# Batch 1 of a fused attention and MLP kernel: segment layout with VectorE turns and GpSimd sums, in place of TensorE transposes

## Chip, cores, metric

One Trainium2 chip, one core. The metric is device time in microseconds of one execution, the median of several runs. Every kernel was timed in rounds against the kernel before on the same chip. "Faster" or "slower" needs 2%.

## The reference

```python
# q, k, v: (8, 8, 576, 64) f32: batch, heads, tokens, head width
q_lm = q.reshape(B, H, 32, 18, D).mean(axis=3)        # 32 landmarks, each the mean of a segment of 18 tokens
k_lm = k.reshape(B, H, 32, 18, D).mean(axis=3)
A, Bm, C = sm(q, k_lm), sm(q_lm, k_lm), sm(q_lm, k)   # sm: softmax of the scaled product
Z = Bm.T / (norm1(Bm) * norminf(Bm))
for _ in range(6):
    Z = 2 * Z - Z @ Bm @ Z                            # pseudo-inverse of Bm, step by step
x = heads_side_by_side(A @ Z @ C @ v)                 # (8, 576, 512)
xn = (x - mean(x)) / sqrt(var(x) + 1e-6) * g_ln
out = x + relu(xn @ w_ch1) @ w_ch2                    # 512 -> 2048 -> 512
```

The eight batches are independent up to `x`. The MLP runs over blocks of 128 tokens, four blocks to a group, and a block can start when its tokens are out of the attention. TensorE therefore always has two streams: attention of a coming batch, and the MLP of batches already done, which the code puts between attention steps with `fill(n)`.

## The kernel before: the parts that matter here

There are two ways to make the attention's operands. Batches 0 and 1 are loaded in a layout that TensorE transposes (`pst`, nine in 0.67 us at 28.07 us), and TensorE sums the landmarks too (`pss`). Batches 2 to 7 are loaded in the segment layout, where a partition holds one head's one segment. VectorE turns such a tile (`STREAM_TRANSPOSE` of 128x576, 0.76 us each in the trace). The k landmarks are summed on VectorE (`add_up`) and the q landmarks on GpSimd, called POOL here (in batches 5 to 7 the k landmarks too).

```python
def load_seg(src, b, u, queue, turned=False):          # segment layout
    t = stage.tile([P, SEG, D], FP32, name="stg", tag="stg")
    rows = src[b, 4 * u:4 * u + 4].rearrange("h (l j) d -> (h l) j d", j=SEG)
    for o, i_ in ((0, 64), (64, 0)) if turned else ((0, 0),):
        n = 64 if turned else P                        # turned: two DMAs of 64 partitions
        keep(queue.dma_start(out=t[ds(o, n), :, :], in_=rows[ds(i_, n), :, :]))
    return t

class Coming:                                          # a set of coming batches, segment layout
    def load(self, i, queue=nc.sync):
        ...
        self.stg[i] = load_seg(..., turned=(nm == "v" and u % 2 == 1))   # v of odd units is turned
    def cast(self, i):
        ...
        pool.tensor_copy(out=t[:], in_=stg[:])         # f32 -> f16
        if nm == "q" or self.k_by_pool:                # landmark sum: five adds on POOL
            for o, x, y in (...):
                pool.tensor_tensor(out=o, in0=x, in1=y, op=ALU.add)

def attention(bs):                                     # batches 0 and 1
    ...
    for j in range(NJ):
        TR(pst[:, j, :], n16[:, j, :, :], ident16[:])  # nine transposes to a tile ...
    dve.tensor_copy(out=t[:], in_=pst[:])              # ... and a copy (VectorE or ScalarE)
    sums()                                             # nine matmuls for the landmarks: pss
    yield

def attention2(bs, c):                                 # batches 2 to 7
    psb = p1([P, W, LM], "psb")                        # first scores: lmq and lmk must be there
    ...

# order of the program
for i in range(HID // W1N):
    load_w1(i)
load_v(1)
...
scale_w1(0, (1, 2, 3)); ...; scale_w1(1); scale_w1(2)  # W1 times g, mostly on POOL
run(a0); fill(4); run(a1); fill(4); ...                # a0, a1: attention of batches 0 and 1, step by step
cast_v(1)
fetch_w2()                                             # 16 loads, 16 casts on POOL
run(a1); fill(16); settle()
sets = [Coming((2,)), Coming((3, 4)), Coming((5, 6), True), Coming((7,), True)]
for i, _ in enumerate(a1):
    fill(5 if i < 9 else 7)
    ...
```

The output stores go through the same SP queue as the loads. The kernel does not hold them to program order (no `keep` around them): the compiler places them.

The softmax here doesn't subtract the row's maximum and nothing guards it: scores larger than these inputs give would overflow.

Of the kernel before, what the change touches and what calls it, by code (L numbers as in the profile page):

```python
# [16 lines left out]
P = 128  # L17
# [3 lines left out]
def kernel(  # L21
# [35 lines left out]
    nat = ctx.enter_context(tc.tile_pool(name="nat", bufs=8))  # L57

# [28 lines left out]
    raw = {0: {}, 1: {}}  # L87

    def load_qk(b):
        for u in range(U):  # L90
            raw[b]["q", u] = load(q, b, u, nc.sync)
            raw[b]["k", u] = load(k, b, u, nc.sync)

    def load_v(b):
        for u in range(U):
            raw[b]["v", u] = load(v, b, u, nc.sync)
# [12 lines left out]
    def cast_qk(b, u, nm, engine):  # L109
        t = nat.tile([P, NJ, 2, D], FP16, name="nat", tag="nat")  # L110
        engine.tensor_copy(out=t[:].rearrange("p j r d -> p r j d"), in_=raw[b][nm, u][:])
        nat_tiles[b, nm, u] = t

    def cast_v(b):
        natv_of[b] = natv = natv_buf[b % NV]
        for u in range(U):
            pool.tensor_copy(out=natv[:, 2 * u:2 * u + 2, :, 0:D], in_=raw[b]["v", u][:])
# [6 lines left out]
    keep(nc.sync.dma_start(out=g_sb[:], in_=moe_g_ln.rearrange("(c p) -> p c", p=P)))  # L124
# [5 lines left out]
    make_identity(nc, ident16)  # L130

# [51 lines left out]
    cast_v(0)  # L183
    bones = const.tile([P, 4, 32], FP16, name="bones")
    for u in range(U):
        for nm in ("q", "k"):
            cast_qk(0, u, nm, dve)
        if u == 0:

            dve.tensor_copy(out=bones[:], in_=mask4[:, :, None].broadcast_to([P, 4, 32]))  # L190
            for i, t in enumerate(zcbd_buf):
                dve.tensor_copy(out=t[:, :, D], in_=(mask4t if i in (3, 5) else mask4)[:])


    load_qk(1)
    for u in range(U):
        for nm in ("q", "k"):
            cast_qk(1, u, nm, pool)

# [3 lines left out]
    xpool = ctx.enter_context(tc.tile_pool(name="xpool", bufs=16))  # L203
# [14 lines left out]
    def scale_w1(i, by=(0, 1, 2, 3)):  # L218
        for c in by:
            o, i_ = w1_16[:, c, ts(i, W1N)], w1_stg[i, c // 2][:, ts(c % 2, W1N)]  # L220
            if c == 0:
                dve.tensor_scalar(out=o, in0=i_, scalar1=g_sb[:, c:c + 1],
                                  scalar2=None, op0=ALU.mult)
            else:
                pool.tensor_scalar(out=o, in0=i_, scalar1=g_sb[:, c:c + 1],
                                   scalar2=0.0, op0=ALU.mult, op1=ALU.add)
# [10 lines left out]
    for i in range(HID // W1N):  # L237
        load_w1(i)
    load_v(1)


# [242 lines left out]
    class Coming:  # L484
        def __init__(self, bs, k_by_pool=False):
            self.bs, self.k_by_pool = bs, k_by_pool
            self.units = [(b, u) for b in bs for u in range(U)]
            pairs = [(w, w + 1) for w in range(0, len(self.units), 2)]
            self.parts = [(nm, w) for pair in pairs for nm in ("k", "q") for w in pair]
            self.parts += [("v", w) for w in range(len(self.units))]  # L490
            self.jobs = []
            for i, (nm, w) in enumerate(self.parts):
                if nm != "v":
                    self.jobs.append((self.turn, i))
                if nm == "k" and not k_by_pool:
                    self.jobs.append((self.add_up, i))
            self.done, self.turned, self.lms = 0, set(), []
            self.stg, self.n16, self.sums, self.xT, self.lm = {}, {}, {}, {}, {}
# [22 lines left out]
        def cast(self, i):  # L521
# [7 lines left out]
            if nm == "v":  # L529
                natv_of[b] = natv_buf[b % NV][:].rearrange("p a j e -> p (a j) e")  # L530
                assert b - NV in v_used
                pool.tensor_copy(out=natv_of[b][:, ds(SEG * u, SEG), 0:D], in_=stg[:])
                return
# [3 lines left out]
            if nm == "q" or self.k_by_pool:  # L537
                s = asum.tile([P, NJ, D], FP32, name="asum", tag="asum")
                s16 = asm.tile([P, D], FP16, name="s16", tag="s16", bufs=8)
                self.sums[i] = s16  # L540
                for o, x, y in ((s[:], t[:, 0:9, :], t[:, 9:18, :]),
                                (s[:, 0:4, :], s[:, 0:4, :], s[:, 4:8, :]),
                                (s[:, 0:2, :], s[:, 0:2, :], s[:, 2:4, :]),
                                (s[:, 0, :], s[:, 0, :], s[:, 8, :]),
                                (s16[:], s[:, 0, :], s[:, 1, :])):
                    with nc.allow_low_precision("sums are rounded once, to fp16"):
                        pool.tensor_tensor(out=o, in0=x, in1=y, op=ALU.add)
# [264 lines left out]
    def store(j, ot, cols=ds(0, DM), queues=(nc.sync, nc.sync)):  # L812
        for i in range(2):
            b, c = divmod(2 * j + i, NJ)
            half = ot[ds(64 * i, 64), cols]
            if b < 2:
# [126 lines left out]
    a0, a1 = attention((0,)), attention((1,))  # L943

    def run(*who):
        for a in who:
            next(a)

    warm(50, 128)
    for _ in range(4):  # L950
        run(a0)
        warm(3, 256)
    run(a0)
    warm(1, 512)
    run(a0)
    warm(1, 512)
    run(a0)
    warm(2, 512)
    for it in range(6):
        run(a0)  # L960
        warm(1, 512)
        if it == 5:
            scale_w1(0, (0,))
    run(a0)
    warm(2, 512)
    run(a0, a0)
    warm(3, 512)
    run(a1)
    warm(1, 512)
    scale_w1(0, (1, 2, 3))  # L970
    fill(1)
    warm(2, 512)
    fill(1)
    warm(2, 512)
    scale_w1(1)
    scale_w1(2)
    run(a0)
    fill(4)
    run(a1)
    fill(4)  # L980
    run(a0)
    fill(2)
    run(a1)
    fill(4)
    for _ in a0:
        pass
    fill(2)
    run(a1)
    fill(4)
    run(a1)  # L990
    fill(4)
    cast_v(1)
    fetch_w2()
    run(a1)
    fill(16)
    settle()


    sets = [Coming((2,)), Coming((3, 4)), Coming((5, 6), True), Coming((7,), True)]
# [11 lines left out]
    def next_cast():  # L1011
        if to_cast:
            c, i = to_cast[0]
            nm, w = c.parts[i]
            if nm != "v" or c.units[w][0] - NV in v_used:
                to_cast.pop(0)
                if cast_before:
                    next_load()
                cast_before.append(i)
                c.cast(i)  # L1020

    for _ in range(6):
        next_load()
    for i, _ in enumerate(a1):
        fill(5 if i < 9 else 7)
        settle()
        next_cast()
        if 5 <= i < 11:
            sets[0].next_job()
    for _ in range(2):  # L1030
        sets[0].next_job()


    counts = [[8, 13, 9] + 6 * [7] + [5] + 3 * [6] + 2 * [9],
              [10, 10, 9, 9, 9, 9] + [9, 9, 8, 8, 8, 8] + [8] + [8, 8, 6, 5] + 6 * [9],
              [12, 12, 15, 15, 15, 13] + 6 * [11] + [10] + 10 * [8],
              [14, 21, 21] + 6 * [10] + [10] + 5 * [9]]
    for c, after, count in zip(sets, sets[1:] + [None], counts):
        for step, _ in enumerate(attention2(c.bs, c)):
            fill(count[step])  # L1040
            settle()
            if late and step >= 3:
# [4 lines left out]
            if after and step >= (5 if after.k_by_pool else 1):  # L1047
# [37 lines left out]
```

## Time and profile before

| | kernel before |
|---|---|
| time, median of 4 runs beside the changed kernel | 330.38 us (329.90 to 331.06) |
| span of the profiled run | 328.4 us |
| TensorE busy | 314.6 us (96%) |
| TensorE idle between 20 and 60 us | 4.26 us |
| mean granted clock | 1.00 |
| batch 1's first scores (`psb`) on TensorE | 37.16 us |
| batch 2's first scores | 63.30 us |
| POOL's first batch-2 cast, its 16th q or k cast | 47.74, 80.70 us |
| wait of TensorE for `xnT` near 142 us | 1.04 us |

Idle time is the stretch less the busy time. These are the engine busy times of the kernel before by longer stretches; the columns are the ones that the prediction explains, TensorE first.

```profile
20.00:60.00 40.00, 35.74 (x448) 24.32 (x448) 32.17 (x72) 20.42 (x39) 35.82 (x58) 1.00 1.05 361
60.00:100.00 40.00, 39.05 (x512) 18.93 (x510) 33.08 (x76) 30.58 (x73) 37.94 (x46) 1.00 0.84 255
100.00:140.00 40.00, 39.09 (x557) 19.38 (x555) 29.93 (x61) 19.14 (x42) 37.32 (x51) 1.00 0.67 185
140.00:170.00 30.00, 28.96 (x515) 13.91 (x513) 12.16 (x29) 14.04 (x30) 22.10 (x33) 1.00 0.55 118
```

TensorE is idle for 4.26, 0.95, 0.91 and 1.04 us in them.

### The profile page before, as it was taken

What the parts mean: (1) busy time and instruction counts of PE and PEld (TensorE: products, weight loads), DVE (VectorE), ACT (ScalarE), POOL (GpSimd) and SP (SyncE); (2) the same over time, 40 slices, a digit from 0 to 9 for tenths busy, and PEclk for the clock granted to TensorE, in tenths of its full rate; (3) what the DMA queues carried; (4) which work ended last, traced back from release to release, by engine and by line L of the source; (5) the groups of instructions that cost most, each with busy time, mean ns of one, the idle gap of its engine ahead of it and who ended that gap; (6) DMA issues with size and microseconds to landing.
All of it is one profiled execution on the core that took longest, in us unless ns stands there. A gap on an engine that the chain in (4) does not pass through costs nothing.

```text
span 328.4 us, 8241 instructions
## 1 busy us (share of the span) xinstructions
PE 314.6 (96%) x3408; PEld 163.0 (50%) x3408; DVE 176.7 (54%) x396; ACT 150.9 (46%) x304; POOL 154.6 (47%) x240
## 2 busy tenths in 40 slices
PE   8879899999999999989999999999999999999995
PEld 8537764454445544434545445454444444444443
DVE  2658869879966588864228568822557120010012
ACT  2426762739961561867304664364046107305600
POOL 3489889999999999989900025200014000000000
PEclk9999999999999999999999999999999999999999
DMA  7999999998598683698022203230242125032023
GB/s 276 350 361 360 383 401 291 317 359 250 212 209 226 186 225 109 163 278 128 4 66 59 43 16 80 66 66 2 64 103 27 32 64 98 0 72 60 0 49 79
DMA packets 36917, 50.34 MB, mean 153 GB/s; under 512 B 18320, under 2 KB 22672, under 8 KB 36880
## 3 DMA queue, kind: packets, MB, share of 16 engines
q1 hardware_dynamic: 36720, 49.69, 53.1%
q8 instruction: 26, 0.43, 0.6%
q10 hardware_dynamic: 160, 0.13, 0.2%
q14 instruction: 11, 0.09, 0.1%
HBM read 36.70 MB, written 9.44 MB: 141 GB/s over the span
## 4 chain that ended last, share of the span: by engine, by line
PE 58%; POOL 17%; DVE 6%; DMA 4%; issue 3%; ACT 2%; SPq 0%; POOLq 0%
PE psh L73 27%; PE pso L73 25%; POOL asum L67 9%; POOL nat L67 4%; POOL natv L67 2%; DMA out_dram<-ot 2%; POOL xn L67 2%; PE psy L73 1%; ACT xn L67 1%; DMA stg<-in_v_dram 1%; PE pscv L73 1%; DVE xT L67 1%; DVE ebd L67 1%; POOL s L67 1%; DMA xnT<-xn 1%
## 5 line engine op out<-in xcount | busy, mean ns | idle before, releaser
L73 PE MATMUL psh<-xnT,w 128*128 128x512 f16 (+1 forms) x640 | 134.2, 358 | 1.0 <-DMA xnT<-xn 1.0
L73 PE MATMUL pso<-w,hT 128*128 128x512 f16 (+1 forms) x592 | 133.0, 374 | 0.0
L67 ACT ACTIVATE hT<-psh 128x512 f16<-128x512 f32 x144 | 84.7, 597 | 94.8 <-PE psh L73 94.6
L73 PEld LDWEIGHTS <-w 128*128 128x128 f16 x640 | 59.4, 98 | 56.0 <-issue 3.0
L73 PEld LDWEIGHTS <-hT 128*128 128x128 f16 x592 | 56.0, 98 | 57.8 <-issue 0.9
L67 DVE SCALAR_TENSOR_TENSOR ot<-pso,rstd,xblk 128x512 f32<-128x512 f32 (+1 forms) x37 | 27.1, 732 | 79.0 <-PE pso L73 78.9
L67 POOL CAST nat<-stg 128x1152 f16<-128x1152 f32 x28 | 32.9, 1185 | 3.8 <-DMA stg<-in_k_dram 1.2
L67 POOL TENSOR_TENSOR asum<-asum 128x256 f32<-128x256 f32 (+2 forms) x54 | 28.3, 523 | 4.2
L67 DVE TENSOR_TENSOR xblk<-psy,rcpd 128x512 f32<-128x512 f32 (+1 forms) x40 | 27.6, 691 | 1.7
L67 POOL TENSOR_TENSOR asum<-nat 128x576 f32<-128x576 f16 x18 | 24.9, 1381 | 1.5
L67 DVE SCALAR_TENSOR_TENSOR st<-st,psn 128x192 f16<-128x192 f16 (+3 forms) x36 | 14.2, 395 | 19.1 <-PE psn L73 19.1
L67 POOL TENSOR_SCALAR xn<-xblk,mvg 128x512 f16<-128x512 f32 x14 | 9.6, 695 | 30.3 <-ACT junk L67 30.3
L67 POOL CAST natv<-stg 128x1152 f16<-128x1152 f32 x16 | 18.1, 1150 | 9.6 <-DMA stg<-in_v_dram 9.6
L67 POOL TENSOR_SCALAR negm<-mvg 128x1 f32<-128x1 f32 x14 | 2.7, 191 | 41.7 <-DVE mvg L67 40.2
L67 DVE TENSOR_TENSOR ebd<-st,mask 128x256 f16<-128x256 f16 (+1 forms) x30 | 21.4, 715 | 1.0
L67 DVE STREAM_TRANSPOSE xT<-nat 128x576 uint32<-128x576 uint32 x24 | 18.2, 760 | 0.8 <-POOL nat L67 0.8
L73 PE MATMUL psy<-zcbd,ea 128*128 128x260 f16 (+1 forms) x80 | 15.9, 276 | 1.3 <-DVE zcbd L67 1.1
L67 ACT ACTIVATE ea<-psea 128x576 f16<-128x576 f32 x12 | 7.2, 648 | 17.8 <-PE psea L73 17.8
L73 PE MATMUL idle<-zeros 128*128 128x128 f16 (+2 forms) x82 | 14.0, 325 | 1.1 <-DVE eps_ln L167 1.1
L73 PEld LDWEIGHTS <-ea 128*128 128x128 f16 (+1 forms) x80 | 7.3, 100 | 11.9 <-issue 4.2
L67 DVE RECIPROCAL rcpd<-psy 128x8 f32<-128x8 f32 (+1 forms) x40 | 7.8, 195 | 9.9 <-PE psy L73 9.6
L67 ACT ACTIVATE junk<-xblk 128x512 f16<-128x512 f32 x14 | 8.8, 625 | 9.3 <-DVE xblk L67 9.1
(109 smaller groups left out, 265.5 us busy)
## 6 DMA issues: line engine op xcount, KB each, us to landing
stg<-in_q_dram SPq DMA_DIRECT2D x16, 576.0 KB, 6.2
stg<-in_k_dram SPq DMA_DIRECT2D x16, 576.0 KB, 6.0
out_dram<-ot SPq DMA_DIRECT2D x70, 128.0 KB, 2.4
stg<-in_v_dram SPq DMA_DIRECT2D x10, 576.0 KB, 8.2
w1stg<-in_moe_w_ch_dram SPq DMA_DIRECT2D x16, 256.0 KB, 6.0
w2stg<-in_moe_w_ch_dram SPq DMA_DIRECT2D x16, 256.0 KB, 5.4
stg<-in_v_dram SPq DMA_DIRECT2D x12, 288.0 KB, 5.7
xnT<-xn SPq DMA_TRANSPOSE x28, 3.2
```

The lines of the kernel that those rows point to most:

```text
L67: return lambda *args, **kw: keep(getattr(self.engine, op)(*args, **kw))
L73: keep(nc.tensor.matmul(o, l, r, start=start, stop=stop, tile_position=(rb, cb), skip_group_check=(skip or cb != 0)))
```

## The change

The intent: TensorE is the full engine, so take batch 1's 72 transposes and landmark matmuls off it and give the work to VectorE (turns) and POOL (sums), as in the later batches. The start is tidied too: the g vector is loaded by rows and transposed on TensorE, half of a v cast goes from POOL to ScalarE (ACT), and so do 14 W1 scalings, six from POOL and all eight of VectorE. Not shown below are new fill counts of the later sets. The core of the diff, cuts marked:

```diff
-    keep(nc.sync.dma_start(out=g_sb[:], in_=moe_g_ln.rearrange("(c p) -> p c", p=P)))
+    g_rows = xpool.tile([P, DM], FP32, name="g_rows", tag="xblk")[0:KCH, 0:P]
+    keep(nc.sync.dma_start(out=g_rows, in_=moe_g_ln.rearrange("(c p) -> c p", p=P)))
...
-            if c == 0:
-                dve.tensor_scalar(out=o, in0=i_, scalar1=g_sb[:, c:c + 1], ...)
+            if c == 0 or c == 1 and i != 1 and i != 2:
+                act(o, i_, AF.Copy, scale=g_sb[:, c:c + 1])
...
-    a0, a1 = attention((0,)), attention((1,))
+    a0 = attention((0,))
+    sets = [Coming((1,), ""), Coming((2,), "q", 6), Coming((3, 4)), Coming((5, 6), "qk", 5),
+            Coming((7,), "qk", 5)]
...
+    fill(4); s1.next_job(); fill(8); s1.next_job()      # turns on VectorE
+    for _ in a0: pass
+    fill(4); s1.next_job(); s1.next_job(); fill(2)
+    for i, (nm, w) in enumerate(s1.parts):
+        if nm == "q":
+            s1.sum_by_pool(i)                           # two landmark sums, after the W1 scalings
+            ...
+    for _ in range(2):                                  # v casts of batch 1
+        c, i = to_cast.pop(0)
+        c.cast(i)
+    fill(4)
...
     fetch_w2()
     for _ in range(6):
         next_load()
-    counts = [[8, 13, 9] + 6 * [7] + [5] + 3 * [6] + 2 * [9],
+    counts = [[12, 8, 10] + 6 * [5] + [5] + 5 * [7],
+              [8, 13, 9] + 6 * [7] + [5] + 3 * [6] + 2 * [9],
```

(The added lines of the order of the program are put together here. In `counts`, each number is how many MLP matmul groups follow an attention step.)

## The prediction

> **What bounds the kernel now.** I read the page's busy shares first, then the engine busy times by stretch of 10 us, then the order of time on TensorE and on GpSimd, then the chain that ended last and the packed DMA records.
>
> ```profile
> PE 314.6 (96%) x3408; PEld 163.0 (50%) x3408; DVE 176.7 (54%) x396; ACT 150.9 (46%) x304; POOL 154.6 (47%) x240
> ...
> 20.00:30.00 10.00, 8.08 (x88) 5.45 (x88) 8.16 (x19) 3.44 (x7) 9.42 (x19) 1.00 1.10 349
> 30.00:40.00 10.00, 8.58 (x138) 7.24 (x137) 8.01 (x21) 7.88 (x15) 9.05 (x15) 1.00 1.05 383
> ...
> 130.00:140.00 10.00, 10.00 (x54) 5.11 (x53) 8.43 (x20) 7.34 (x21) 9.69 (x14) 1.00 0.65 171
> ```
>
> The columns of the stretches are PE, weight load, DVE, ACT, POOL, clock, DMA share, GB/s. TensorE is busy 96% of the span, so the end is set by its work plus its few idle spots. But POOL's 47% is an average of two halves: it is full (9.0 to 9.7 of 10) from 20 to 140 us and nearly idle afterwards. The DMA share is about 1 up to 50 us. There are therefore three limits early on, and only TensorE late.
>
> ```profile
> 24.45 0.42 PE L73 MATMUL pss<-pm,nat 128*128 128x64 f16 x9
> ...
> 28.07 0.67 PE L77 MATMUL pst<-ident,nat 128*128 128x128 f16 x9
> 28.57 0.43 PE L73 MATMUL pss<-pm,nat 128*128 128x64 f16 x9
> 28.84 1.04 PE L73 MATMUL psh<-xnT,w 128*128 128x256 f16 x8
> ...
> 37.16 0.22 PE L73 MATMUL psb<-klm,qbd 64*32 64x32 f16 x8 [0.84 <-DVE qbd L67]
> ```
>
> Batch 1's transposes (pst) and landmark sums (pss) stand here between MLP matmuls (psh); nine of each take 0.77 us from start to next start (28.07 to 28.84). The batch's first scores (psb) begin at 37.16 us, after 44 of the 128 narrow psh matmuls of the first block group.
>
> ```profile
> 21.50 11.91 POOL L67 TENSOR_SCALAR w<-w1stg,g_sb 128x256 f16<-128x256 f32 x24
> 33.78 1.15 POOL L67 CAST natv<-stg 128x1152 f16<-128x1152 f32 x1 [0.38 <-DMA stg<-in_v_dram]
> 35.28 1.15 POOL L67 CAST natv<-stg 128x1152 f16<-128x1152 f32 x1 [0.35 <-DMA stg<-in_v_dram]
> 36.37 10.53 POOL L67 CAST w<-w2stg 128x512 f16<-128x512 f32 x16
> 47.74 1.15 POOL L67 CAST nat<-stg 128x1152 f16<-128x1152 f32 x1 [0.84 <-PE psn L73]
> 51.83 1.32 POOL L67 TENSOR_TENSOR asum<-nat 128x576 f32<-128x576 f16 x1
> 53.23 1.66 POOL L67 TENSOR_TENSOR asum<-asum 128x256 f32<-128x256 f32 x3
> 54.96 0.32 POOL L67 TENSOR_TENSOR s<-asum 128x64 f16<-128x64 f32 x1
> ...
> 139.19 2.84 DMA xnT<-xn
> 142.17 1.02 PE psh L73 x4
> ```
>
> POOL's order in time shows the program order that the change cuts into: W1 scaling, v casts, W2 casts, batch 2. One landmark sum is the five adds from 51.83 to 55.28, about 3.5 us with gaps. The last two lines are from the chain: until 139 us the chain runs through POOL, and TensorE waits 1.04 us for its product at 142.17. POOL is a second bound with no slack.
>
> [...] the old g load left 512 packets of 4 bytes, took 9.7 us to land, and the DMA rate fell from about 405 GB/s to 66 GB/s for a microsecond near 13 us in the packet records. [...] here 72 transposes need eight copies (three on DVE at 746 ns, five on ACT at 1111 ns). [...] No pair of equal adds is in this trace; its 128x576 add took 1381 ns.
>
> **The change part by part.**
>
> 1. TensorE, batch 1. Removed after 27.2 us: three pst/pss groups (0.77, 0.76, about 0.9 with the copy wait left out), psb and psc 0.84 (37.16 to 38.00), psse and pscv 1.00 (41.59 to 42.59), psn, psa and pszc about 1.6: 5.9 us. Added, read from batch 2, which has this form already: psb and psec 1.13 (its 0.38 us of waiting left out), psse 0.13, pscv 1.19 and 0.75 less tails = 1.8, psea 0.64, six psn and pszc about 0.7: 4.4 us. Net -1.5 us on the full engine. The first transpose group lay among filler matmuls and counts nothing.
>
> 2. The start. In DVE's order, zcbd of batch 0 stands behind a W1 scaling that waited 0.93 us for W1 data at 21.10. The scaling goes to ACT, and half of batch 0's last v cast too (it held pscv 0.51 us at 14.59). I take -1.2 us for the first MLP matmul (27.2 to about 26.0). The g load's hole is worth about 1.2 us of DMA time to everything behind it: the last W1 piece lands at about 31.1 instead of 32.3.
>
> 3. POOL. Two landmark sums are added, 2 x 3.5 = +7.0 us. Six scalings go to ACT, 6 x 0.50 = -3.0; half of a v cast, -0.6. Casts of batch 1 stay. Net about +3.5 us on an engine with no slack.
>
> 4. Where the added sums lie. In program order they come behind the last W1 scaling. That needs the last W1 piece, so the three scalings saved don't bring it forward by more than the DMA does: 31.1 + 2 x 0.5 = 32.1. Sums end at 32.1 + 7.0 = 39.1; the small DVE turns bring psb of batch 1 to about 39.6, where it was 37.16. By then 40 psh matmuls stand before it in TensorE's order instead of 44. TensorE is idle for much of the time before: from 26.0 to 39.6 it has only 40 x 0.109 + 1.6 for psxt and psy = 6.0 us of useful work, and the long wait for q sums is not filled. ACT, which gets 14 scalings (about 0.40 us, estimated from 0.26 us for 128 and 0.65 us for 576 columns), four centerings at most and the ReLUs, runs to about 35 us and isn't the last.
>
> 5. Balance for TensorE at the end of batch 1: psb later by 39.6 - 37.2 = +2.4; four narrow matmuls fewer done, +0.4; work from psb on 4.4 against 3.4 (0.84 + 1.0 + 1.6), +1.0: about +3.8 us behind.
>
> 6. POOL behind that: v casts end at 41.4, W2 casts at 41.4 + 10.5 = 51.9 against 46.9; the waits of 0.84 and two of 0.28 us that it had before batch 2's casts go away, so the lag is about 4 us. It has little to give back until 140 us, so the xnT at 142.17 is late by much the same 4 us. The two lags are not added: TensorE is late by 3.8 when it comes to wait for it.
>
> After 142 us both versions have the same MLP work (13.81 us per 64 matmuls) and the same attention. The sum is 330.5 + 4 = 334.5 us.
>
> **The rivals.**
>
> A: TensorE's saving comes through. If the q sums are early enough, or the retuned fill counts cover them, what remains is -1.5 (work) - 1.2 (start) - about 1 (the old stalls of 0.58 and 0.84 at 33.9 and 37.16 go away): 326.5 to 327 us. For it speaks the 96% of TensorE, and that the fill counts were clearly set by hand: twelve steps of MLP are put behind psb, which one would rather put ahead of it had it been seen waiting. Against it speaks POOL's order of time.
>
> B: POOL becomes the bound up to 140 us, twice: at psb of batch 1 and at the xnT near 142 us. That is the sum above, 334.5 us. [...]
>
> C: the POOL lag is absorbed. POOL's casts also wait for buffers that DVE frees at TensorE's pace; then only the first lag counts, less slack, and the start pays for some of it: about 331.5 us.
>
> D: ACT becomes the bound in 22 to 40 us by its scalings and ReLUs. It had 7.88 of 10 busy in 30 to 40 already. It would hold psh by 1 to 2 us, but psb waits longer for POOL, so it adds nothing to B.
>
> **Range and chances.** My working says B; the hand-set counts speak for A or C, and my error on the POOL end time is some 2 us. Weighing B at 50%, C at 30%, A at 20% gives 334.5 x 0.5 + 331.5 x 0.3 + 326.8 x 0.2 = 332.1, so 332 us, range 326 to 337. Faster than 323.9 us would need more than A gives: 6%. Slower than 337.1 needs B with slow adds: 10%. Within 2%: 84%.
>
> **What would show it right or wrong.** Right: in TensorE's order of time psb of batch 1 starts near 39.6 us after a wait of 3 us or more for a landmark turn or s16; POOL's ten adds end near 39 us; W2 casts end near 52 us; a wait on xnT of more than 1 us near 145 us; first MLP matmul near 26 us; no 4-byte hole in the DMA. Wrong: psb starts before 37.5 us, or the waits at xnT vanish although POOL's W2 casts end 4 us later (then C), or TensorE's waits before 65 us sum to less than before (then A).

(Statements on the hardware that no trace or run of this case shows are cut out, here and in the expectations of e0 and e10. No term of the sum is among them: it came to 330.5 + 4 = 334.5 us. What is gone with them is a case of rival B, 336 to 338 us, for adds on POOL that are slower than the shortest of 1.27 us; the 10% for "B with slow adds" rests on it (1381 ns in the prediction is the mean of POOL's 18 adds of 128x576). The reason given for slow adds was not shown, and in the changed kernel's first profile batch 1's two 128x576 adds took 1.27 us each (34.03 and 37.51 us).)

## The result

The changed kernel took **339.47 us** (337.41 to 342.04, 4 runs) beside 330.38 us of the kernel before. The ratio is 1.028, 95% interval 1.0225 to 1.0336: slower. The prediction said 332.0 with a range up to 337.

The profiled run of the changed kernel is its slowest, 342.04 us; the repeat e0_after gives a profile of an ordinary one, and I name it where they differ. First the page of the changed kernel: busy line, and of the 40 slices (8.5 us each) TensorE and its clock.

```profile
PE 316.3 (93%) x3424; PEld 162.1 (48%) x3424; DVE 178.9 (53%) x396; ACT 155.0 (46%) x318; POOL 156.1 (46%) x245
...
PE   8876299899999998969999999999999999999995
...
PEclk9999679999999999998999999999999999999999
```

TensorE's busy time did not fall, it rose by 1.7 us, and slice 5 (34 to 42.5 us) is nearly empty. The clock row has a 6 and a 7 right there. The stretches of the changed kernel, short ones first:

```profile
30.00:40.00 10.00, 2.75 (x32) 2.16 (x31) 5.16 (x9) 6.23 (x15) 7.25 (x12) 0.84 1.04 276
40.00:50.00 10.00, 8.80 (x161) 6.26 (x161) 5.98 (x18) 4.36 (x10) 9.84 (x18) 0.65 0.64 214
```

```profile
20.00:60.00 40.00, 28.38 (x423) 19.75 (x416) 25.30 (x56) 21.84 (x47) 31.80 (x52) 0.87 0.96 301
60.00:100.00 40.00, 38.37 (x425) 18.68 (x423) 35.46 (x75) 25.73 (x59) 34.27 (x45) 1.00 0.83 238
100.00:140.00 40.00, 38.76 (x638) 18.42 (x637) 29.48 (x60) 18.48 (x38) 37.16 (x49) 1.00 0.82 207
140.00:170.00 30.00, 26.74 (x261) 12.49 (x259) 16.25 (x39) 20.30 (x49) 27.91 (x42) 0.94 0.75 163
```

Idle is now 11.62, 1.63, 1.24 and 3.26 us: 7.4 us more before 60 us, 2.2 us more around the `xnT` product, 1.0 us between. With the 1.7 us of extra busy time (mostly matmuls at a lower clock) that makes 12.3 us, close to the 11.9 us by which the span grew (340.3 against 328.4); outside these stretches it idles a little less. Between 30 and 40 us TensorE was busy 8.58 us before, 2.75 us now. Of these 5.8 us, 2.2 are the transposes and sums that left. The larger part, 4.1 us, is MLP matmuls (`psh`: 5.98 us before, 1.91 now): they were ready, but in program order they now stand behind the scores that TensorE waits for. So the work that left had filled waits, and nothing was put in its place.

TensorE's order of time in the changed kernel (start, length, what; in brackets the idle time before it and who ended it):

```profile
37.73 0.24 PE L74 MATMUL psb<-lmk,lmq 32*32 32x32 f16 x8 [3.54 <-DVE lmq L68]
41.20 0.22 PE L74 MATMUL psb<-lmk,lmq 32*32 32x32 f16 x4 [3.23 <-DVE lmq L68]
...
41.27 1.13 PE L74 MATMUL psec<-xT,lmq 32*32 32x512 f16 x28
42.34 5.10 PE L74 MATMUL psh<-xnT,w 128*128 128x256 f16 x24
...
152.51 3.21 PE L74 MATMUL psh<-xnT,w 128*128 128x512 f16 x8 [3.26 <-DMA xnT<-xn]
```

The narrow `psh` that follow batch 1's first scores in the kernel before:

```profile
38.00 3.67 PE L73 MATMUL psh<-xnT,w 128*128 128x256 f16 x32
```

Two waits of over 3 us stand before batch 1's scores. After them everything on TensorE is slow: 28 `psec` take 1.13 us, and 24 narrow `psh` take 5.10 us, that is 213 ns each, where the kernel before took 3.67 us for 32, 115 ns each. The same happens at 152.51 us. This is the step that I had not thought of at all. In the trace the granted clock falls to 0.50 at both places: from 36.9 to 47.1 us, that is 2.7 us into the wait of 3.54 us (0.65 on average between 40 and 50 us), and from 152.9 to 156.3 us, 0.4 us after the end of the wait for `xnT` of 3.26 us. In the run e1 below it is down from 32.4 to 35.8 us. How long a wait brings it down is not one number here. Over all profiled runs, 14 waits at the `xnT` product lasted 2.69 to 3.26 us; after 12 the clock fell, after two (2.92 us in e16, 2.94 in e9) it did not, and after none of those up to 1.83 us. Early in e1 it fell with no wait above 2.06 us: TensorE was busy 0.93 of the 3.5 us from 29.0 to 32.5 us, and the clock was 0.50 after that. In e17 it was busy the same 0.93 us, with the same wait of 2.06 us, and the clock stayed at 1.00. What decides between the two, no run shows.

POOL's order of time in the changed kernel:

```profile
33.13 0.93 POOL L68 TENSOR_SCALAR w<-w1stg,g_sb 128x256 f16<-128x256 f32 x2 [1.91 <-DMA w1stg<-in_moe_w_ch_dram]
34.03 1.27 POOL L68 TENSOR_TENSOR asum<-nat 128x576 f32<-128x576 f16 x1
...
40.58 0.32 POOL L68 TENSOR_TENSOR s<-asum 128x64 f16<-128x64 f32 x1
40.85 2.23 POOL L68 CAST natv<-stg 128x1152 f16<-128x1152 f32 x2
43.02 9.17 POOL L68 CAST w<-w2stg 128x512 f16<-128x512 f32 x16
52.61 1.15 POOL L68 CAST nat<-stg 128x1152 f16<-128x1152 f32 x1 [0.42 <-DMA stg<-in_k_dram]
...
85.57 1.15 POOL L68 CAST nat<-stg 128x1152 f16<-128x1152 f32 x1 [3.52 <-DMA stg<-in_q_dram]
```

The last W1 piece reached POOL at 33.13 us after a wait of 1.91 us; I had put its landing at 31.1. Part of the reason may be seen in the packet records. v of batch 1 now comes in the segment layout, and its odd unit is "turned": two DMAs of 64 partitions. While they are in flight the 4608-byte packets of v take 364 to 465 ns (medians by microsecond, 31 to 34 us) in place of 182, the 2048-byte packets of the W2 load 155 to 158 ns (32 to 34 us) in place of 87, and the rate falls to 173 to 197 GB/s between 31 and 34 us from about 390. The kernel before shows the same drop (229 to 246 GB/s between 52 and 57 us, 406 at 50 us), when batch 2's turned v comes in. It was there to be seen. But it does not explain the 2 us: the ordinary run e0 has the same slow stretch (143 to 195 GB/s; 279 on average from 30 to 40 us, in the first profile 276, in the kernel before 383), and there the last W1 scaling begins at 31.74 us. The rest belongs to this slow run alone, and its cause is open.

The lag of POOL against the kernel before is 4.9 us at batch 2's first cast (52.61 against 47.74) and 9.6 us at its 16th q or k cast (90.28 against 80.70). It grows on the way (in e0 less, from 4.9 to 7.0 us). One place stands out, the wait of 3.52 us for a load at 85.57 (in e0 1.11 us). The SP queue's order of time in the changed kernel, then in the kernel before:

```profile
67.80 7.37 SPq L813 DMA_DIRECT2D out_dram<-ot  x6
75.27 1.30 SPq L106 DMA_DIRECT2D stg<-in_k_dram  x1
```

```profile
63.54 1.25 SPq L817 DMA_DIRECT2D out_dram<-ot  x2
64.89 0.53 SPq L105 DMA_DIRECT2D stg<-in_q_dram  x1
```

Six output stores, each waiting for its MLP result, now stand in the queue ahead of loads that POOL needs. So there are four suspects: the waits and the clock, the split v load, POOL's added sums, and the stores ahead of the loads. What each is worth can't be read from one trace, since POOL and TensorE wait for each other.

### The profile page after: what moved, and what is told of

Its sections match the earlier page's. It is cut to its first block, busy times and chain, and to the rows that moved or that the text cites. A ratio compares the mean times of both kernels' runs of the same rounds, so it can differ in the third digit from the quotient of the medians.

```text
span 340.3 us, 8292 instructions
## 1 busy us (share of the span) xinstructions
PE 316.3 (93%) x3424; PEld 162.1 (48%) x3424; DVE 178.9 (53%) x396; ACT 155.0 (46%) x318; POOL 156.1 (46%) x245
## 4 chain that ended last, share of the span: by engine, by line
PE 58%; POOL 20%; DMA 13%; DVE 4%; issue 2%; SPq 1%; POOLq 0%; DVEq 0%
PE psh L74 28%; PE pso L74 25%; POOL asum L68 11%; DMA stg<-in_v_dram 6%; POOL nat L68 5%; DMA w1stg<-in_moe_w_ch_dram 4%; POOL natv L68 2%; POOL xn L68 2%; PE pscv L74 2%; PE psy L74 1%; DMA stg<-in_q_dram 1%; POOL s L68 1%; DMA xnT<-xn 1%; DVE ebd L68 1%; DMA w2stg<-in_moe_w_ch_dram 1%
## 5 line engine op out<-in xcount | busy, mean ns | idle before, releaser
L74 PE MATMUL psh<-xnT,w 128*128 128x512 f16 (+1 forms) x640 | 136.6, 366 | 3.8 <-DMA xnT<-xn 3.3
L74 PEld LDWEIGHTS <-w 128*128 128x128 f16 x640 | 61.3, 100 | 60.3 <-DMA xnT<-xn 3.6
L68 POOL TENSOR_TENSOR asum<-asum 128x256 f32<-128x256 f32 (+2 forms) x60 | 31.6, 527 | 4.7
L68 POOL TENSOR_TENSOR asum<-nat 128x576 f32<-128x576 f16 x20 | 26.9, 1346 | 1.5
L68 POOL TENSOR_SCALAR xn<-xblk,mvg 128x512 f16<-128x512 f32 x14 | 9.7, 693 | 32.5 <-ACT junk L68 32.5
L68 POOL CAST natv<-stg 128x1152 f16<-128x1152 f32 (+1 forms) x16 | 17.7, 1118 | 11.1 <-DMA stg<-in_v_dram 8.8
L68 DVE STREAM_TRANSPOSE xT<-nat 128x576 uint32<-128x576 uint32 x28 | 21.2, 761 | 0.2 <-POOL nat L68 0.2
L68 ACT ACTIVATE ea<-psea 128x576 f16<-128x576 f32 x14 | 8.3, 648 | 21.0 <-PE psea L74 21.0
L74 PEld LDWEIGHTS <-ea 128*128 128x128 f16 (+1 forms) x80 | 7.5, 101 | 11.5 <-issue 3.8
```

Source lines behind the costliest of these rows:

```text
L68: return lambda *args, **kw: keep(getattr(self.engine, op)(*args, **kw))
L74: keep(nc.tensor.matmul(o, l, r, start=start, stop=stop, tile_position=(rb, cb), skip_group_check=(skip or cb != 0)))
```

## The experiments

All have 3 rounds (e12 5), on three chips, each beside the kernel before on the same one, and it took 330.2 to 330.5 us. "Net lateness" below is the start of batch 2's first scores less 63.30 us (kernel before), less 1.73 us for the eight more `pso` matmuls (0.216 us each) that the changed kernel's fill counts put ahead of that point: work done early is not time lost.

### e0_after: the changed kernel again

No edit.

> The changed kernel again, as the yardstick for the runs of this call. Both theories: 337 to 342 us, 1.02 to 1.035 of before. If its runs again spread over 4 us or more while before spreads over 1 us, the spread belongs to the kernel, which the clock theory explains [...] and the theory of late sums alone does not.

339.21 us (337.62 to 340.83), 1.027 (1.0231 to 1.0308). Its profile has the two waits at `psb` at 1.96 and 3.08 us, net lateness 6.3 us, and the `xnT` wait again 3.26 us with slow `psh` after it. In the slowest run, profiled first, the net lateness was 8.9 us. The runs spread over 3.2 us and those of the kernel before over 0.7, a little under the 4 us that I had set as the sign of the clock theory (that the waits lower the clock, and so cost twice). TensorE, then POOL's last W1 scaling, in e0:

```profile
36.53 0.22 PE L74 MATMUL psb<-lmk,lmq 32*32 32x32 f16 x8 [1.96 <-DVE lmq L68]
39.84 0.21 PE L74 MATMUL psb<-lmk,lmq 32*32 32x32 f16 x4 [3.08 <-DVE lmq L68]
...
40.97 4.62 PE L74 MATMUL psh<-xnT,w 128*128 128x256 f16 x24
...
31.74 0.94 POOL L68 TENSOR_SCALAR w<-w1stg,g_sb 128x256 f16<-128x256 f32 x2 [1.04 <-DMA w1stg<-in_moe_w_ch_dram]
```

### One suspect at a time: e2, e4, e1, e3, e8

**e2_vwhole: v of batch 1 in one DMA of 128 partitions.** The result is wrong (relative error 0.34: the odd unit's halves are not swapped); the work is the same.

```diff
-    turned=(nm == "v" and u % 2 == 1))
+    turned=(nm == "v" and u % 2 == 1 and b != 1))
```

> The changed kernel with batch 1's second v tile loaded in one DMA over 128 partitions, not turned, instead of two over 64 each; batch 1's numbers come out wrong on purpose. DMA theory (a DMA onto 64 partitions runs at half the rate and holds up the last W1 piece and W2): from 32 to 38 us about 390 GB/s instead of 160 to 260, last W1 scaling on POOL at about 31.5 us instead of 33.13, second psb near 39.6 instead of 41.2, W2 issues end near 43 instead of 46.9; time lower by 2 to 3 us. Late sums by POOL's own work alone: W1 is ahead in the queue, so psb and the time stay.

338.36 us, 1.0238 (1.0194 to 1.0282): not told apart from e0. POOL's order of time in e2:

```profile
31.34 0.93 POOL L68 TENSOR_SCALAR w<-w1stg,g_sb 128x256 f16<-128x256 f32 x2 [0.48 <-DMA w1stg<-in_moe_w_ch_dram]
```

The last W1 scaling begins at 31.34 us and POOL's sums end at 39.13, near my prediction's 31.1 and 39.1. But with the split load an ordinary run is hardly later: 31.74 and 39.54 in e0, and 31.33 and 39.12 in e19 below. So the 33.13 us of the first profile isn't shown to come from the split load, and the DMA theory is not borne out here. (The load in one DMA is itself not slow: e2 moved 377 GB/s from 25.3 to 33.7 us, e0 296 in the same slice.) What the split load does delay is v itself (casts at 34.98 and 37.60 us in e6, at 32.48 and 33.91 in e9, whose v is whole). The waits at `psb` are 1.96 and 1.63 us (e0: 1.96 and 3.08); the clock had already dropped after a wait of 2.05 us at 31.28, so the first scores begin 1 us later than in e0.

**e4_fill: twelve MLP steps put ahead of the scores instead of behind them.**

```diff
+    fill(12)
-    counts = [[12, 8, 10] + 6 * [5] + ...
+    counts = [[6, 6, 6] + 6 * [5] + ...
```

> The changed kernel with 12 MLP steps (24 narrow psh matmuls) moved from behind the first scores of batch 1 to ahead of them. Theory that TensorE idles there only by its program order: the first wait shrinks from 3.5 us to about 1, these 24 matmuls run at full clock (2.7 us), time lower by 3 to 5 us, to about 335.5. Rival, ACT or the W1 pieces bind in that stretch: the 24 matmuls can't run any earlier, the wait moves to them, and the time falls by less than 1 us.

338.34 us, 1.0242 (1.0219 to 1.0266). Now the scores wait only 0.52 us, the clock is 1.00 between 40 and 50 us, and net lateness falls from 6.3 to 3.4 us. Little of these 3 us reaches the end. The `xnT` product comes at 147.95 us (e0: 150.17), still after a wait of 2.69 us.

**e1_warm: keep the clock up with idle matmuls in the waits.**

```diff
+                if bs == (1,):
+                    warm(14, 512)        # ahead of each unit's psb
```

> The changed kernel with 14 matmuls of zeros put into each of the two waits ahead of batch 1's psb. Nothing that matters comes earlier. Clock theory (the waits cost twice: once as idle time and once as matmuls at a lower granted clock after them): granted clock 0.95 or more from 40 to 50 us instead of 0.65, the 24 narrow psh matmuls after psec take about 2.7 us instead of 5.1, psec 0.7 instead of 1.1, and the time falls by about 3 us to 336.5. Late sums alone: the waits end when they end, no change, 339.5 within 1 us.

340.97 us, 1.0323 (1.0274 to 1.0373): no gain. TensorE's order of time in e1:

```profile
39.85 3.20 PE L74 MATMUL idle<-zeros 128*128 128x512 f16 x14
42.98 0.21 PE L74 MATMUL psb<-lmk,lmq 32*32 32x32 f16 x5
...
43.65 2.79 PE L74 MATMUL psh<-xnT,w 128*128 128x256 f16 x24
```

The 24 `psh` take 2.79 us in place of 5.10, and the clock is 1.00 between 40 and 50 us in place of 0.65, so the long wait does cause the slow clock. But the idle matmuls overran the wait: the scores begin at 42.98 us, later than in either profile of the changed kernel (41.20, 39.84), and two gaps of 1.32 and 1.54 us follow in which TensorE waited for nothing that the profile shows. My 14 was too many. Nor did they keep the clock up throughout: it was down from 32.4 to 35.8 us, ahead of the scores. The experiment shows the cause of the slow matmuls and not what they cost.

**e3_dvesum: batch 1's q sums on VectorE** (`add_up`, as its k sums already are) instead of POOL.

```diff
-                if nm == "k" and nm not in by_pool:
+                if (nm == "k" or bs == (1,)) and nm not in by_pool:
-    (the two s1.sum_by_pool calls)
```

> The changed kernel with the two q landmark sums of batch 1 made by DVE from the turned tiles, as it makes the k sums (1.34 us each), in place of ten adds on POOL. Theory POOL-order (the 7 us of adds ahead of the v and W2 casts hold up psb, W2, the loads behind W2 in the SP queue, and so all of POOL up to the xnT wait): second psb at about 38.5 us instead of 39.7 to 41.2, W2 casts begin near 34.5 instead of 43, batch 2's first cast near 47 instead of 52.6, xnT wait near 143 to 144 us instead of 150 to 152; time about 331 to 332. Rival, TensorE's order and MLP counts of the new set cost by themselves: time still 336 or more.

341.06 us, 1.0322 (1.0281 to 1.0362): no gain, against all that I expected. POOL has 6 us less to do and its first batch-2 cast comes at 49.94 us (changed kernel: 52.61), but then it waits for loads. POOL's order of time in e3:

```profile
79.27 1.15 POOL L68 CAST nat<-stg 128x1152 f16<-128x1152 f32 x1 [2.29 <-DMA stg<-in_k_dram]
85.01 1.15 POOL L68 CAST nat<-stg 128x1152 f16<-128x1152 f32 x1 [4.60 <-DMA stg<-in_q_dram]
```

What POOL gained it handed back at the SP queue. And TensorE is no earlier for it: net lateness is 8.1 us (e0: 6.3), with waits of 2.59 and 1.85 us at the scores and the slow matmuls behind them.

**e8_loads: four of batch 2's loads issued ahead of the W2 loads.**

```diff
+    for _ in range(4):
+        next_load()
     fetch_w2()
-    for _ in range(6):
+    for _ in range(2):
         next_load()
```

> The changed kernel with four of batch 2's loads put ahead of W2's sixteen in the SP queue. If the lag of POOL beyond its own added work comes from loads that stand behind W2's waits for buffers: batch 2's first cast without a DMA wait, about 1.5 us earlier at its fourth cast (60 instead of 61.6), time lower by 1 to 2 us. If W2 is pushed back by as much, or later waits take it up: no change, 339.

339.81 us, 1.0295 (1.0261 to 1.033): nothing. W2's data, and so POOL's W2 casts, only come later (43.9 to 54.9 us), and batch 2's first cast is at 54.84 us.

### Several together: e6, e9, e10, e13, e14

**e6_dvesum_fill** is e3 and e4 together.

> DVE sums as in the run before and the 12 MLP steps ahead of psb. If both the POOL order and TensorE's idle stretch count: 328 to 330 us, at or a little under before, since 1.5 us of TensorE work and 1.2 us of start are saved. If only the POOL order counts: as the run before.

337.37 us, 1.0228 (1.0195 to 1.0261). Net lateness 2.7 us, and the `xnT` wait is 3.07 us at 146.16 us.

**e9_d_f_vwhole** is e6 with e2 as well (numbers wrong).

> DVE sums, 12 MLP steps ahead of psb, and batch 1's second v tile in one DMA over 128 partitions, unturned (wrong numbers on purpose). With the sums off POOL, its v casts are bound by the landing of v (34.98 and 37.60 us against 33.78 and 35.28 before). DMA theory: second v cast at about 34.5, W2 casts from 35.7, batch 2's first cast near 47.5 instead of 50.4, xnT wait ends at 143 to 144 instead of 146.2, time 332 to 333. Rival (the half-rate DMA is made up for later): 337.

338.05 us, 1.0231 (1.0203 to 1.0259). POOL is now earlier than in the kernel before at batch 2's first cast (46.46 against 47.74) and 7 us later at the 16th (87.67), because of waits for loads. **e10_d_f_twoq** is e6 with the two halves of v issued from two queues (SP and ACT), and two of the loads behind them moved.

```diff
-            keep(queue.dma_start(out=t[ds(o, n), :, :], in_=rows[ds(i_, n), :, :]))
+            keep((nc.scalar if turned and b == 1 and o == 0 else queue).dma_start(
+                out=t[ds(o, n), :, :], in_=rows[ds(i_, n), :, :]))
```

> DVE sums, 12 MLP steps ahead of psb, and the two 64-partition halves of batch 1's second v tile issued from two queues (SP and ACT)[...]; numbers right. If halves at once make up for the half rate: as the run with v whole, 332 to 333. If the rate belongs to each DMA [...]: as without, 337[...].

338.51 us, 1.0247 (1.0194 to 1.0301). It doesn't help: the v casts come at 35.38 and 37.18 us, in e6 at 34.98 and 37.60.

**e13_dvesum_lf** is e3, **e14_d_f_lf** is e6, each with the next cast and its load put ahead of the fill in the steps of batches 1 and 2, so that loads stand ahead of stores in program order.

```diff
+            early = c in sets[:2]
+            if early and after.done < len(after.parts):
+                next_cast()
             fill(count[step])
```

> The kernel with DVE sums, and in the sets of batch 1 and 2 each next load and cast is put ahead of the step's MLP work, so that loads stand before that step's output stores in the SP queue. With DVE sums alone POOL lost its 7 us of adds but then waited 2.29 and 4.60 us near 79 and 85 us for loads that stood behind six stores, and the time stayed at 341. Theory queue-order (the in-order SP queue ties POOL to late TensorE work): those two waits shrink to under 2 us together, xnT wait ends near 148 instead of 152.5, time about 337. Rival (POOL is merely waiting out TensorE, which is late anyway): the waits move elsewhere, time 340 to 341.

340.01 us, 1.0282 (1.0244 to 1.032). That is what the rival said, no change. The 16th cast is earlier, at 84.87 us, but the next one is still at 101.27; a wait of 2.45 us is left, now for VectorE.

> DVE sums, 12 MLP steps ahead of psb, and loads ahead of the stores. There the two load waits were already small (0.96 us), so queue-order expects little: 336.5 to 337.5 against 337.4. If it falls below 335, loads behind stores cost there as well.

335.59 us, 1.0167 (1.013 to 1.0203): the lowest so far, though its interval touches that of e6, and the two profiled spans differ by 0.4 us only. `xnT` at 145.88 us, wait 2.74 us.

### The stores ahead of the loads: e16, e15, e17

e13 left the place of the stores to the compiler. These three hold them back, by issuing the stores of blocks 0 to 3 only at step 6 of batch 2's set:

```diff
     def store(j, ot, ...):
+        if held is not None and j < 4:
+            held.append((j, ot))
+            return
...
+            if c is sets[1] and step == 6:
+                while held:
+                    put(*held.pop(0))
```

**e16_hold** is the changed kernel with it, **e15_dvesum_hold** is e3 with it, **e17_d_f_v_hold** is e9 with it (numbers wrong).

> The changed kernel with the output stores of blocks 0 to 3 held back to step 6 of batch 2's set. Theory (loads stand behind stores in the SP queue): POOL's casts near 75 to 90 us come some 3 us earlier (lag against the kernel before at its 15th and 16th cast 6.4 us instead of 9.6), xnT wait ends near 149 instead of 152.5, time about 336. Rival (POOL's lag is its own work, loads would be there anyway): no change, 339 to 340.

337.62 us, 1.0222 (1.0201 to 1.0243): between theory and rival. It is not clear that the stores did it: POOL's 17th cast comes at 99.53 us, in e0 at 99.90 (the 16th at 86.38, in e0 at 87.66). In its profile the wait for `xnT` (2.92 us) did not bring the clock down, as it did in e0; of the 2.6 us by which its profiled run is shorter, 1.65 are that, and the product was 0.95 us earlier.

> e3_dvesum with the same stores held back. Theory: POOL's waits of 2.29 and 4.60 us for loads near 76 to 85 us vanish, its 16th cast comes at 82 to 84 us, the xnT wait ends near 145 to 146 us, time about 334. Rival (the loads are late for another cause): as e3_dvesum, 340 to 341.

340.62 us, 1.0307 (1.0281 to 1.0332). The waits of 2.29 and 4.60 us for loads are gone, as the theory says. The time did not move, which it doesn't say.

> e9_d_f_vwhole (numbers wrong on purpose, v of batch 1 is not in the right order) with the same stores held back: all four suspected causes are taken away. Theory: POOL is as early as in the kernel before (16th cast near 80 us), the xnT wait ends at 141 to 142 us, time 330 to 331. Rival (something else also delays POOL): xnT wait ends past 146 us, time over 334.

338.13 us, 1.0256 (1.0223 to 1.0288). My theory fell here. All four suspects are taken away up to 60 us (the wait at the scores is 1.22 us, and the clock is 1.00, by luck: e9, the same but for the stores, has the same early waits, and there it dropped at 32.4 us), POOL's 16th cast is at 79.06 us, earlier than in the kernel before, and the time is still 2.6% over. What took the place of the waits for loads is seen in POOL's order of time in e17:

```profile
84.16 1.14 POOL L68 CAST natv<-stg 128x1152 f16<-128x1152 f32 x1
90.38 0.69 POOL L68 TENSOR_SCALAR xn<-xblk,mvg 128x512 f16<-128x512 f32 x1 [5.08 <-ACT junk L68]
```

POOL waits 5.08 us for the layer-norm statistics that ACT makes (`junk`). In ACT's order they stand behind ReLUs (`hT`) of MLP matmuls, and those of the next block behind batch 2's first attention output (`psy`). Both come when TensorE has got that far: that `psy` starts at 90.00 us, 85.66 in the kernel before, and 1.7 of these 4.3 us are the eight `pso` put ahead. e15 has the same wait, 3.43 us at 94.44. So POOL is not simply late by its own work: when it is early, it waits for TensorE. That TensorE in turn is late by its own early waits is how I read the trace. TensorE in e17, three of its waits in order of time:

```profile
31.12 0.38 PE L78 MATMUL psxt<-ident,xn 128*128 128x128 f16 x4 [2.06 <-ACT hT L68]
...
49.96 0.39 PE L74 MATMUL psh<-xnT,w 128*128 128x256 f16 x2 [0.98 <-issue]
...
57.61 0.23 PE L74 MATMUL pszc<-st,bmbd 128*128 128x64 f16 x2 [0.91 <-DVE bmbd L68]
```

Even here TensorE idles 9.65 us between 20 and 60 us (busy 30.35 of 40) against 4.26, at full clock: for ACT at 31 us, for batch 1's last turns, for VectorE in the pseudo-inverse steps. In the kernel before, the transposes lay in the first of these places.

### The start alone, and POOL's load at the xnT product: e7, e12, e19, e20

**e7_start** is the kernel before with only the start of the change: g by rows, half a v cast on ACT, the first W1 scaling on ACT.

```diff
+    g_rows = xpool.tile([P, DM], FP32, name="g_rows", tag="xblk")[0:KCH, 0:P]
+    keep(nc.sync.dma_start(out=g_rows, in_=moe_g_ln.rearrange("(c p) -> c p", p=P)))
...
+    scalar.copy(natv_buf[0][:, 3, :, 0:D], raw[0]["v", 1][:, 1])
...
-            scale_w1(0, (0,))
+            act(w1_16[:, 0, ts(0, W1N)], w1_stg[0, 0][:, ts(0, W1N)], AF.Copy, scale=g_sb[:, 0:1])
```

> The kernel before with the parts of the change that concern the start alone: g by rows and a small transpose, half of batch 0's last v cast on ACT, the first W1 scaling on ACT; batch 1 stays as it was. My step for the start: first MLP matmul about 1.2 us earlier, time 329 to 329.5. Rival: what is won at the start is waited away at the W1 pieces or at xnT (POOL ends at the same time), time 330.4.

329.82 us, 1.0002 (0.9963 to 1.004): the same. TensorE is over a microsecond ahead early (22.75 us at batch 1's transposes, 23.95 before), and then waits 1.83 us for `xnT` at 141.73 us instead of 1.04 at 142.17. The start's gain was mostly waited away, for POOL.

**e12_start_kdve** adds to e7 that two of the k sums of batches 5 and 6 go from POOL to VectorE, 7 us off POOL ahead of that product.

```diff
-            if nm == "q" or self.k_by_pool:
+            if nm == "q" or self.k_by_pool and w not in self.by_dve:
-    sets = [..., Coming((5, 6), True), ...
+    sets = [..., Coming((5, 6), True, (2, 3)), ...
```

> The kernel before with the start's parts of the change alone (e7_start), and two of POOL's k sums of batches 5 and 6 moved to DVE (7 us less POOL work ahead of the xnT product). Theory (the start's gain of 1.2 us is lost at the wait for xnT, where POOL is last): the wait of 1.83 us near 142 us vanishes, 328.0 to 328.8 us. Rival (it is lost elsewhere, or DVE's longer reductions delay TensorE): 329.8 us or more.

**328.06 us**, 0.9929 (0.9905 to 0.9952), correct (its profile is of its slowest run, 329.42 us): under the kernel before with the whole interval below 1, though by 0.7% only, which is "the same" by the 2% measure. The wait for `xnT` is gone from TensorE's order of time; the product starts at 141.44 us without one. The sums were not run without the start, so how the gain divides between them is open.

**e19_after_kdve** is the changed kernel, **e20_d_f_lf_kdve** is e14, each with the same two sums moved.

> The changed kernel with two of POOL's k sums of batches 5 and 6 moved to DVE, as in e12. Theory (the loss is two parts: TensorE's own lag of some 5 us from its early waits, and the wait on xnT with its clock drop): the xnT wait of 3.26 us near 152 us and the half-clock matmuls after it vanish, about 335 us. Rival 1 (POOL's lag at xnT is the whole loss): 331 us or less. Rival 2 (TensorE would only wait elsewhere): 339 us.

336.06 us, 1.0185 (1.0159 to 1.021), as the two-part theory said (335). The product and its wait in e19:

```profile
147.99 1.89 PE L74 MATMUL psh<-xnT,w 128*128 128x512 f16 x8 [0.16 <-DMA xnT<-xn]
```

The wait is 0.16 us, the matmuls after it run at full speed (1.89 us for 8 in place of 3.21), and the time falls by 3.2 us against e0. So about 3.2 of the 8.8 us that the changed kernel loses lie at this product. (In the profiled runs 0.9 us of it may be chance: net lateness is 5.4 us against 6.3 before the moved sums come.)

> e14_d_f_lf (the best repair of the segment form, 335.59 us) with the same two sums on DVE. Theory: its xnT wait of 2.74 us and the slow matmuls after it vanish, about 331.5 us. Rival 1: under 328 us (POOL was the only thing left). Rival 2: 335 us or more.

333.73 us, 1.0113 (1.009 to 1.0135), "the same" by the 2% measure, though the whole interval is above 1; I expected 331.5. The wait at `xnT` is down to 0.43 us. The best version of the segment layout is still 3.4 us over the kernel before. Its TensorE, early on:

```profile
20.00:60.00 40.00, 31.71 (x444) 20.58 (x443) 32.05 (x67) 21.69 (x47) 29.03 (x46) 0.96 1.04 322
```

8.29 us idle against 4.26 is 4.0 us more, about what is still missing. The waits for ACT (1.29 us at 24.43, 2.05 us at 31.67) and for the layer-norm product `xnT` of the first blocks are in every version of the change, and no run took them away.

### All versions of the changed kernel side by side

| run | what | time, us | net lateness, us | `xnT` product, us (wait) |
|---|---|---|---|---|
| e0 | the change | 339.21 | 6.3 | 150.17 (3.26) |
| e1 | idle matmuls | 340.97 | 11.0 | 154.41 (0.98) |
| e2 | v whole (wrong) | 338.36 | 5.7 | 149.42 (3.13) |
| e4 | fill ahead | 338.34 | 3.4 | 147.95 (2.69) |
| e3 | sums on VectorE | 341.06 | 8.1 | 152.46 (2.83) |
| e8 | batch 2's loads ahead | 339.81 | 6.7 | 150.87 (3.23) |
| e15 | e3, stores held | 340.62 | 7.2 | 151.14 (3.06) |
| e16 | stores held | 337.62 | 6.5 | 149.22 (2.92) |
| e6 | e3 and e4 | 337.37 | 2.7 | 146.16 (3.07) |
| e9 | e6, v whole (wrong) | 338.05 | 6.0 | 149.85 (2.94) |
| e10 | e6, v from two queues | 338.51 | 7.1 | 150.85 (2.98) |
| e13 | e3, loads ahead | 340.01 | 7.4 | 150.96 (2.93) |
| e17 | e9, stores held (wrong) | 338.13 | 3.4 | 147.42 (3.24) |
| e14 | e6, loads ahead | 335.59 | 3.5 | 145.88 (2.74) |
| e19 | e0, POOL relieved late | 336.06 | 5.4 | 147.99 (0.16) |
| e20 | e14, POOL relieved late | 333.73 | 3.7 | 145.84 (0.43) |

(Times are medians; the other columns are of the one profiled run.) The time goes with both columns: it needs TensorE in time before 65 us and POOL in time at 145. The profiled spans say it more sharply. From the start of the `xnT` product to the end it is 186.1 to 186.3 us in all eight profiles with full clock there (the kernel before, e1, e7, e9, e12, e16, e19, e20), and 187.6 to 187.9 in eleven of the twelve with the clock drop (189.0 in e17, where it stays down longer). So a profiled run loses just what it is late at that product, plus usually 1.6 us for the drop. In the first profile 10.3 and 1.6 make the whole 11.9 us; in e20 it is 3.7 us and no drop, and e14 differs from e20 by the drop alone. No repair of one alone brings more than 3.2 us.

## Why the prediction was wrong

The prediction's own sum said 4 us slower (its rival B, 334.5 us), it was 9 us, and the weighing with A and C took the number further off, to 332. B's mechanism was right, and most of its signs came (scores at 39.84 us after a wait of 3.08, sums ending at 39.5, W2 casts at 52.2, a long wait for `xnT`); what it costs was too small by half. By its steps:

1. **TensorE's saving, -1.5 us: it came, and did not help.** TensorE's busy time is 314.8 us in e0, 313.6 in e9 and 313.5 in e20, against 314.6, but the changed kernel's has half-clock time in it. In e9, 16 `psh` took 3.56 us at 32.23 where they take 1.91 at full clock, so its work alone is about 312 us (an estimate from these numbers). What the transposes left behind was idle time: 2.75 us busy between 30 and 40.
2. **The start, -1.2 us: right, and worth nothing.** The first MLP matmul came at 25.99 us, predicted 26.0; the hole in the DMA rate near 13 us is gone (403 and 389 GB/s from 11 to 13 us, 151 and 197 before). e7 shows that the gain alone ends in the wait for `xnT`.
3. **POOL, +3.5 us: too high.** POOL's busy time rose from 154.6 us to 156.1 (156.8 in e0), though gaps between the adds are not counted in it. The sums are as long as said (34.03 to 40.9 us for two), and the W2 casts end at 52.2 us, predicted 51.9.
4. **Scores at 39.6 us: right in an ordinary run (39.84), 41.20 in the slow one.** There the last W1 piece was 2 us late, and why is open: with the split v load the last scaling begins at 31.74 us in e0 and 31.33 in e19, without it at 31.34 in e2.
5. **TensorE late by 3.8 us: this is the step that failed.** It was 8.9 us in the first profile (6.3 in e0). In the first: scores later 4.0 us (predicted 2.4), four fewer `psh` 0.4 (0.4), half clock after the waits 2.7 (none; 0.44 for `psec`, and 24 `psh` until the next instruction took 4.93 us where e1 took 2.63), more waits for VectorE in batch 1's pseudo-inverse and first outputs 0.8 (none; 1.53 us against 0.74). That leaves 0.9 for the added work, said to be 1.0. In e0 the same sum is 2.7 for the scores, 0.4 for the `psh`, 2.3 for the half clock (`psec` 0.44; the 24 `psh` 4.45 us against 2.63), 0.5 for the waits, and 0.4 is left: in an ordinary run the missing term is the half clock. I had counted only how late the wait ends, not what a wait of 3 us does to the clock, nor that batch 1's later steps would wait too.
6. **POOL about 4 us late, and so `xnT` too: mis-sized.** POOL was 4.9 us late at batch 2's first cast and 9.6 us late at the 16th (7.0 in e0). I held POOL for the source of the lag; in e17 it waits for TensorE's output once its own delays are taken away. The product was late by 10.3 us (152.51 against 142.17; 8.0 in e0), and the wait there brought a second clock drop of some 1.6 us, which I had left out: "after 142 us both versions have the same" was wrong by that.

Three readings of the profile in the prediction were loose. POOL is not 9.0 to 9.7 busy all the way from 20 to 140 us: it is 8.43 of 10 between 40 and 50 and 8.92 between 50 and 60, so it had some slack there. Nor is it nearly idle afterwards (22.10 of 30 us between 140 and 170). And the hole in the DMA rate lies at 11.5 to 12.5 us rather than 13.

**The rivals.** A (326.5) and C (331.5) got half of my weight, A for hand-set fill counts: an argument about what the author must have seen, with nothing in the profile behind it. e4 shows that the counts were in fact not the best. D, ACT, was called harmless: the waits for ACT at 24 and 31 us (1.29 and 2.05) are in every version, and are the first candidates for what remains. A rival that no run tested stands right there: in e0 ACT does two W1 scalings (0.89 us at 30.13) just ahead of the `hT` (30.92) that ends the wait of 2.05 us, where in the kernel before `hT` follows the centring at once (30.36). No run took the scalings off ACT again.

**Where the loss went, as far as shown.** Of 8.8 us (e0), 3.2 are at the `xnT` product (e19). Better fills, sums on VectorE and loads ahead of stores together are worth 3.6 us (e14), and 5.5 us with the POOL relief (e20). The split v load and the stores ahead of the loads are real waits that cost nearly nothing by themselves, since another wait stood behind each. The last 3.4 us are all lost before the `xnT` product, as e20's 3.7 us of lateness there show. They match TensorE's 4.0 us more of idle time before 60 us; that these idle spots are the cause is argued from the trace of e20, not shown by a run. Open too: the gaps of 0.8 to 1.8 us marked "issue" in some runs, and what part of e16's gain is the stores'.

## What to carry to other kernels

Before taking work off the busiest engine, look at what that engine would do in that time: work that fills a wait for another engine costs nothing there, and taking it away leaves idle time (here 11.62 us between 20 and 60 us in place of 4.26), unless other ready work stands ahead of the wait in program order (e4 put some there and took 3 us off the early lag). When the change makes a wait on TensorE of about 3 us, add the matmuls at a clock of 0.50 after it to its price (here 12 of 14 waits of 2.69 to 3.26 us at one product had them). And when a repair removes a wait that the trace shows and the time stays, look for the wait that stands next behind it before calling the first harmless (in e15 waits of 2.29 and 4.60 us for loads were gone, and the time stayed at 340.62 us): when engines wait for each other, a wait shows who was last, not what being early would bring.
